# A decayed-attention and routed-expert kernel: compare table built group by group, ranks counted by matmuls, expert pieces at fixed steps, weights loaded one piece per step

## Chip, cores and metric

The kernel runs on one core of one Trainium2 chip. The metric is the device time in microseconds (us). Five engines work side by side, each through its own instructions in order: PE (TensorE, matmuls and transposes, with PEld for its weight loads), DVE (VectorE), ACT (ScalarE), POOL (GpSimd) and SP, which here only issues transfers (DMA). An instruction that needs another engine's result waits on a semaphore, and everything behind it on the same engine waits with it.

## The reference, cut to what matters

Four batches (B=4), eight heads (H=8), S=768 positions, head width 64, blocks of 64 positions.

```python
for b in range(nb):                                  # blocks of 64 positions
    intra = einsum('bhic,bhjc->bhij', qb, kb) * Dmask   # scores, decayed by lam
    intra = einsum('bhij,bhjd->bhid', intra, vb)
    inter = einsum('bhid,bhde->bhie', qb * lam_pow, kv_state)
    out[:, :, sl] = intra + inter
    kv_state = lam_block * kv_state + einsum('bhsd,bhse->bhde', kb * rev_pow, vb)
# x = out as (B, S, 512); then, per batch:
scores = einsum('bsd,d->bs', x, w_gate)
top_idx = argpartition(-scores[b], 128)[:128]        # the 128 best of 768 rows
ye = maximum(x[b, top_idx] @ w1, 0) @ w2             # 512 -> 1024 -> 512
out[b, top_idx] = x[b, top_idx] + sigmoid(scores)[:, None] * ye
```

All of it is in float32 in the kernel, but for small 0/1 tables.

## The kernel before

The work comes in 24 groups of 128 rows, six per batch (NT=6); a loop makes one **step** per group. F(g) below is the moment at which step g's first matmul, `from_scores(g)`, starts on PE.

Step g holds, in program order: loads of group g+6 (three DMAs of 256 KB, L67, on SP); in steps 0 to 3 two pieces of the expert weights of 512 KB each (`load_weights`, L83 and L86, on SP too); `from_scores(g)` and `outputs(g)` (PE writes the last part of group g, three ACT copies take it to `x_b`, SP stores it, L260); `from_states(g+1)`, `scores(g+1)` and `state_products(g+2)` on PE; `masked(g+1)` and two `next_state` on DVE, each fed by a `decayed` on POOL (L206): the state is a chain DVE, POOL, DVE, POOL through all groups of a batch; `gate_scores(g)` on DVE (L267); the transposes of group g+3 on PE with their ACT copies; `kd` (L143) and `qs` (L163) on POOL. Scores and state products share one PSUM tile `su`, of which there is one; the transposes and all expert results share two PSUM banks (`ps_m`).

When a batch's six groups are done, its routing begins: `rows` transposes all gate scores into one row (L288), `count` compares that row with each of the six score columns on DVE (`cmp`, L305, 128x768, six per batch) and sums up the ranks, `place_of_slots` makes a 0/1 table on DVE (`pick`, L330) and turns it into the 128 row numbers by six small matmuls (L337) and three DVE instructions. `fetch` gathers the rows from the output in memory by an indirect DMA on POOL's queue (L353). The expert is then `gate` (transposes L363), two `hidden` (L392) and `back` (L403), which ends in an indirect DMA that scatters the rows (L412, POOL).

`plan(b)` lays these pieces into later steps, where they stand between the two transposes of the step:

```python
s = (b + 1) * NT + (b < B - 1)
for i, piece in enumerate(counts):
    put(s + i // 2, piece)
s += 2
s = max(s, busy_until[0]); put(s + 1, where); put(s + 2, fetch)
for j, piece in enumerate(pieces):                 # gate, hidden, hidden, back
    put(s + 3 + j, piece)
```

So batch 0 counts in steps 7 to 9, places in 10, fetches in 11 and computes in 12 to 15; batch 1 does the same six steps later; batch 2 fetches in step 23 and computes after the loop; batch 3 does all of it after the loop. The expert's last `back` is written as one piece of eight matmuls.

## Time and profile before

| what | value |
|---|---|
| time, median of 3 runs (lowest, highest) | 235.78 us (235.48, 237.22) |
| the profiled execution: its time, its span in the trace | 238.65 us, 236.9 us |
| mean granted clock of TensorE, share of full speed | 0.848 |
| PE / PEld / DVE / ACT / POOL busy | 167.9 / 137.0 / 103.7 / 65.9 / 107.2 us |
| moved by DMA | 32.24 MB |

Busy times of engines overlap, so they don't add up to the span. A profile row of the timeline reads: start in us, duration in us, engine, source line, operation, what is written from what, count, and in brackets how long the engine sat idle before it and what ended that.

### The profile page before, as it was taken

The page shows a single profiled execution, that of the slowest core. Times are in us where ns is not written, and L with a number is a line of the kernel's source. Part 1 is how long each engine was busy: PE and PEld are TensorE (multiplying, and loading weights), DVE is VectorE, ACT ScalarE, POOL GpSimd, SP SyncE. Part 2 cuts the span into 40 slices and gives each one's busy share as a digit, 9 for nine tenths or more (in the row PEclk, how much of TensorE's full clock was granted, in tenths as well). Part 3 has the DMA queues.
Part 4 walks back from the last instruction along what each step waited for, and adds up shares of the span by engine and source line. Part 5 has one row for each costly group of instructions (what it writes and reads, how often), then busy time and mean ns, then how long its engine had stood idle before and what let it go on. Part 6 is the DMA issues. An engine that isn't in the chain of part 4 may idle for free.

```text
span 236.9 us, 7953 instructions
## 1 busy us (share of the span) xinstructions
PE 167.9 (71%) x3520; PEld 137.0 (58%) x3520; DVE 103.7 (44%) x241; ACT 65.9 (28%) x145; POOL 107.2 (45%) x105
## 2 busy tenths in 40 slices
PE   1869775775178519399999394999991499607991
PEld 1658665664167419298965293889651396207940
DVE  3545441253056983544852734348636180301001
ACT  2333351333043404243342133434311111001100
POOL 1689873656345972946461829664112000220001
PEclk9997997789558976959999869599998579965999
DMA  6999999999899998976573832101102200020001
GB/s 128 220 226 202 203 294 269 237 270 273 212 249 249 244 255 202 230 158 136 136 159 67 191 78 91 45 7 47 47 3 93 84 3 0 0 89 1 3 0 44
DMA packets 80962, 32.24 MB, mean 136 GB/s; under 512 B 75680, under 2 KB 75680, under 8 KB 80928
## 3 DMA queue, kind: packets, MB, share of 16 engines
q1 hardware_dynamic: 80144, 29.63, 53.6%
q0 software_dynamic: 640, 2.10, 3.0%
q8 instruction: 28, 0.46, 0.8%
q14 instruction: 6, 0.05, 0.1%
q10 hardware_dynamic: 144, 0.00, 0.0%
HBM read 24.38 MB, written 7.34 MB: 134 GB/s over the span
## 4 chain that ended last, share of the span: by engine, by line
PE 43%; DMA 21%; issue 13%; DVE 12%; POOL 6%; SPq 2%; ACT 1%; POOLq 1%
DMA kn<-in_k_dram 15%; PE ph L392 10%; PE py L403 9%; DMA xs<-out_dram,tok 6%; PE po L243 4%; PE su L196 4%; PE su L176 4%; DVE cmp L305 4%; PE tp_kT L154 3%; PE po L230 3%; POOL decayed L206 3%; PE tp_qT L154 2%; POOL kd L143 2%; DVE pick L330 2%; DVE p L183 2%
## 5 line engine op out<-in xcount | busy, mean ns | idle before, releaser
L206 POOL TENSOR_TENSOR decayed<-state,decay 128x256 f32<-128x256 f32 x40 | 39.6, 989 | 38.5 <-DVE state L217 32.5
L183 DVE TENSOR_TENSOR p<-su,mask 128x512 f32<-128x512 f32 x24 | 16.6, 691 | 42.0 <-PE su L196 37.0
L143 POOL TENSOR_TENSOR kd<-kn,kpow 128x512 f32<-128x512 f32 x24 | 27.3, 1136 | 16.2 <-DMA kn<-in_k_dram 16.1
L392 PE MATMUL ph<-xsT,w_sb 128*128 128x128 f32 x256 | 32.7, 292 | 1.0 <-ACT xsT L367 1.0
L392 PEld LDWEIGHTS ph<-xsT,w_sb 128*128 128x128 f32 x256 | 32.0, 208 | 1.8 <-ACT xsT L367 1.4
L412 POOL DMA_INDIRECT out_dram<-y,tok x4 | 5.5, 1386 | 60.6 <-DVE y L408 60.6
L163 POOL TENSOR_TENSOR qs<-qT,qpow 128x512 f32<-128x512 f32 x24 | 31.3, 1306 | 3.5 <-ACT qT L158 2.5
L305 DVE SCALAR_TENSOR_TENSOR cmp<-sc_row,sc,earlier 128x768 f32<-128x768 f32 x24 | 28.5, 1229 | 9.7 <-ACT sc_row L293 9.7
L158 ACT COPY qT<-tp_qT 128x512 f32<-128x512 f32 x24 | 14.1, 586 | 60.7 <-PE tp_qT L154 60.7
L403 PE MATMUL py<-w_sb,hs 128*128 128x512 f32 x64 | 28.2, 594 | 0.0
L154 PE MATMUL tp_qT<-ident,qn 128*128 128x128 f32 x96 | 19.2, 332 | 10.1 <-DMA qn<-in_q_dram 10.0
L217 DVE TENSOR_TENSOR state<-su,decayed 128x256 f32<-128x256 f32 x40 | 16.8, 419 | 21.2 <-POOL decayed L206 21.2
L230 PE MATMUL po<-state,qs 64*64 64x64 f32 x704 | 19.6, 237 | 7.9 <-issue 7.8
L176 PE MATMUL su<-qT,kT 64*64 64x64 f32 x768 | 21.1, 249 | 5.4 <-DVE state L217 4.0
L176 PEld LDWEIGHTS su<-qT,kT 64*64 64x64 f32 x768 | 18.1, 159 | 6.8 <-issue 6.6
L230 PEld LDWEIGHTS po<-state,qs 64*64 64x64 f32 x704 | 16.6, 152 | 8.8 <-issue 8.5
L196 PE MATMUL su<-vn,kd 64*64 64x64 f32 x704 | 21.0, 257 | 0.4 <-issue 0.3
L158 ACT COPY kT<-tp_kT 128x512 f32<-128x512 f32 x24 | 14.1, 587 | 20.7 <-PE tp_kT L154 20.5
L243 PE MATMUL po<-vn,p 64*64 64x64 f32 x768 | 18.9, 244 | 1.3 <-DVE p L183 1.3
L403 PEld LDWEIGHTS py<-w_sb,hs 128*128 128x128 f32 x64 | 11.8, 190 | 13.5 <-issue 13.4
L154 PEld LDWEIGHTS tp_qT<-ident,qn 128*128 128x128 f32 x96 | 12.5, 168 | 12.2 <-issue 10.4
L267 DVE CUSTOM_DVE_ANT_0 xg<-x_b,wg_b 128x512 f32<-128x512 f32 x24 | 18.8, 785 | 1.3 <-ACT x_b L259 1.3
(52 smaller groups left out, 164.4 us busy)
## 6 DMA issues: line engine op xcount, KB each, us to landing
qn<-in_q_dram SPq DMA_DIRECT2D x24, 256.0 KB, 4.9
kn<-in_k_dram SPq DMA_DIRECT2D x24, 256.0 KB, 5.2
vn<-in_v_dram SPq DMA_DIRECT2D x24, 256.0 KB, 5.2
out_dram<-x_b SPq DMA_DIRECT2D x24, 256.0 KB, 3.9
w_sb<-in_moe_w_dram SPq DMA_DIRECT2D x8, 512.0 KB, 5.8
wg_b<-in_moe_w_gate_dram SPq DMA_DIRECT2D x1, 256.0 KB, 5.2
xs<-out_dram,tok POOLq DMA_INDIRECT x4, 3.7
out_dram<-y,tok POOLq DMA_INDIRECT x4, 3.5
```

The lines of the kernel that those rows point to most:

```text
L143: nc.gpsimd.tensor_tensor(out=kd[:], in0=loaded[g][1][:], in1=kpow[:].rearrange("p a b -> p (a b)").unsqueeze(2).broadcast_to([128, H, D]) ...
L154: nc.tensor.transpose(tp[:, hp, :], in_=t[:, 2 * hp : 2 * hp + 2, :], identity=ident[:])
L158: nc.scalar.copy(out=dst[:], in_=tp[:])
L163: nc.gpsimd.tensor_tensor(out=qs[:], in0=qTs[g][:], in1=qpow[:].rearrange("p a c i -> p a (c i)"), op=ALU.mult)
L176: nc.tensor.matmul(su[half[c], hh, 0, hp, :], lhsT=kT[half[hh], hp, half[c]], rhs=qT[half[hh], hp, half[c]], start=True, stop=True, skip_g ...
L196: nc.tensor.matmul(su[half[hh], c, 1, hp, :], lhsT=kd[half[c], h, :], rhs=vn[half[c], h, :], start=True, stop=True, skip_group_check=True,)
L206: nc.gpsimd.tensor_tensor(out=t[:], in0=states[n][:], in1=decay[:], op=ALU.mult)
L230: nc.tensor.matmul(po[half[hh ^ c], hh, hp * D : (hp + 1) * D], lhsT=qs[half[hh], hp, half[c]], rhs=states[n][half[hh], hp, :], start=(hp ...
L243: nc.tensor.matmul(po[half[hh ^ c], hh, hp * D : (hp + 1) * D], lhsT=p[half[c], hh, hp, :], rhs=vn[half[c], 2 * hp + hh, :], start=(hp == ...
L305: nc.vector.scalar_tensor_tensor(out=cmp[:], in0=keep["sc_row"][:], scalar=scs[b][:, t : t + 1], in1=earlier[:, (NT - 1 - t) * L : (NT - 1 ...
L392: nc.tensor.matmul(ph[:, i, :], lhsT=w1_sb[:, dc, fs], rhs=xsT[:, dc, :], start=(dc == 0), stop=(dc == NDC - 1),)
L403: nc.tensor.matmul(py[:], lhsT=hs[:, fc, :], rhs=w2_sb[:, fc, :], start=(fc == 0), stop=(fc == NFC - 1),)
```

## The change

It does the following.

- **Routing.** `row(g)` transposes one group's gate scores in every step and ACT copies them into the row tile; `compare(g-1)` on DVE fills that group's part of a 0/1 table `wins` (bf16) against all groups so far, two instructions for the group itself and two more that grow with t, the number of groups before it. `places(b)` sums the table by twelve matmuls with a tile of ones (384 columns each, in two halves) and finds the row numbers with two DVE instructions of 384 elements and a small one. `count`, `place_of_slots` and their tables are gone.
- **Plan.** Pieces stand at fixed steps: for batches 0 to 2 with s=6(b+1): places and fetch in step s+1, gate in s+3, hidden in s+4 and s+5, `back`, now cut into two halves of four matmuls, in s+6 and s+7. For batch 3 places and fetch are in step 24, the rest behind it, two steps after. Steps past 23 come after the loop; there, batch 2's halves of `back` stand before and after batch 3's places.
- **Weights.** One piece of 512 KB per step in steps 1 to 8 in place of two per step in steps 0 to 3.
- **PSUM.** Scores move into the tile `po` of their own group (two of these); state products get a tile `pu`, which also holds the new row transpose. The two shared banks are handed out in turn, and one of them is held from the first half of `back` to the second.
- **Order.** `scores` now stand before `from_states`; `keys_decayed(g+3)` (`kd`) moves from between the two `decayed` of a step to the end of POOL's step.

```diff
+    def row(g, u):
+        b, t = divmod(g, NT)
+        ...
+        pb = u[:, 0, 256 : 256 + L]
+        nc.tensor.transpose(
+            pb, in_=scs[b][:, t : t + 1].broadcast_to([128, 128]), identity=ident[:]
+        )
+        nc.scalar.copy(out=rows_[b][:, t * L : (t + 1) * L], in_=pb)
+    def compare(g):
+        ...
+        nc.vector.scalar_tensor_tensor(
+            out=tie[:], in0=sc_row[:, here], scalar=s, in1=behind[:],
+            op0=ALU.is_le, op1=ALU.mult,
+        )
+        nc.vector.scalar_tensor_tensor(
+            out=wins[:, t, here], in0=sc_row[:, here], scalar=s, in1=tie[:],
+            op0=ALU.is_lt, op1=ALU.max,
+        )
+        if t > 0:
             nc.vector.tensor_scalar(
+                out=wins[:, t, : t * L], in0=sc_row[:, : t * L], scalar1=s, scalar2=None,
+                op0=ALU.is_lt,
+            )
             nc.vector.tensor_tensor(
+                out=wins[:, :t, here], in0=sc_row[:, here].unsqueeze(1).broadcast_to([128, t, L]),
+                in1=sc[:, :t].unsqueeze(2).broadcast_to([128, t, L]), op=ALU.is_le,
+            )
+    def places(b):
+        ...
+        for f in range(2):
+            cnt = bank([128, W], "cnt")
             for t in range(NT):
                 nc.tensor.matmul(
+                    cnt[:], lhsT=ones[:], rhs=wins_[b][:, t, f * W : (f + 1) * W],
                     start=(t == 0), stop=(t == NT - 1),
                 )
+                nc.vector.scalar_tensor_tensor(
+                    out=hit[:], in0=cnt[:], scalar=slot[:, i : i + 1],
+                    in1=token[:, f * W : (f + 1) * W],
+                    op0=ALU.is_equal, op1=ALU.mult, accum_out=part[:, f, i : i + 1],
+                )
     def plan(b):
-        s = (b + 1) * NT + (b < B - 1)
+        last = b == B - 1
+        s = (b + 1) * NT
+        put(s + (not last), lambda: places(b))
         for i in range(NGR):
             s = max(s, busy_until[0])
+            fetch, pieces = expert(b, i)
+            put(s + 1 - last, fetch)
             for j, piece in enumerate(pieces):
+                put(s + 3 - last + j, piece)
+            busy_until[0] = s + len(pieces)
     for g in range(NG):
-        for i in range(2 * g, min(2 * g + 2, n_w)):
-            load_weights(i)
+        if 0 < g <= n_w:
+            load_weights(g - 1)
         if g + 2 < NG:
             decay_state(2 * g + 4)
-        if g + 3 < NG:
-            keys_decayed(g + 3)
         from_scores(g)
         outputs(g)
         if g + 1 < NG:
+            scores(g + 1)
             from_states(g + 1)
         ...
+        if g > 0 and NGR:
+            compare(g - 1)
         if g + 3 < NG:
             transposes(g + 3, "qT", qTs)
             queries_decayed(g + 3)
+            keys_decayed(g + 3)
         for piece in later.pop(g, []):
             piece()
+        u = us.pop(g + 2)
+        if NGR:
+            row(g, u)
         if g + 3 < NG:
             transposes(g + 3, "kT", kTs)
```

Where batch 0's expert ends and batch 1's gather stands, on POOL in step 13 of the changed kernel (`tok_1197` are batch 0's row numbers, `tok_1941` batch 1's; the rows go from step 13 into step 14):

```order
L220 TENSOR_TENSOR decayed<-state,decay 128x256 x2
L174 TENSOR_TENSOR qs<-qT,qpow 128x512
L154 TENSOR_TENSOR kd<-kn,kpow 128x512
L425 DMA out_dram<-y,tok_1197 768x512
L361 DMA xs<-out_dram,tok_1941 128x512
L220 TENSOR_TENSOR decayed<-state,decay 128x256 x2
```

Before, two steps lay between batch 0's scatter (768x512, step 15) and batch 1's gather (step 17), as POOL's rows from one to the other show:

```order
L412 DMA out_dram<-y,tok 768x512
L143 TENSOR_TENSOR kd<-kn,kpow 128x512
L206 TENSOR_TENSOR decayed<-state,decay 128x256
L163 TENSOR_TENSOR qs<-qT,qpow 128x512
L206 TENSOR_TENSOR decayed<-state,decay 128x256
L143 TENSOR_TENSOR kd<-kn,kpow 128x512
L206 TENSOR_TENSOR decayed<-state,decay 128x256
L163 TENSOR_TENSOR qs<-qT,qpow 128x512
L353 DMA xs<-out_dram,tok 128x512
```

Now the gather is issued right behind the scatter, with nothing between them, and the next step's `decayed` stands behind both.

PE's last rows before, from the last group's `from_scores` (`po`, L243) on, are these; both the transposes `pt` and all matmuls `ph` and `py` of batches 2 and 3 come after it, with the six small matmuls of batch 3's `pick` (one pair of rows shown) between them:

```order
L243 MATMUL po<-vn,p 64x64 x16
L363 MATMUL pt<-ident,xs 128x128 x4
L288 MATMUL pb<-ident,sc 128x128 x6
L392 MATMUL ph<-xsT,w_sb 128x128 x32
L403 MATMUL py<-w_sb,hs 128x512 x8
L337 LDWEIGHTS pick
L337 MATMUL pe<-place,pick 128x2
```

The same place in the change (`po`, L252, is the last group's `from_scores`):

```order
L252 MATMUL po<-vn,p 64x64 x16
L400 MATMUL ph<-xsT,w_sb 128x128 x16
L295 MATMUL pu<-ident,sc 128x128
L413 MATMUL py<-w_sb,hs 128x512 x4
L334 LDWEIGHTS ones
L334 MATMUL cnt<-wins,ones 128x384
```

Batch 2's gate and first half of `ph` have moved ahead of the last group, into the loop, and the counting of batch 3 (twelve such pairs of `ones` and `cnt`) stands behind the first half of batch 2's `py`.

## Rows read from the trace of the kernel before

**Rows 1.** The page: the span, and busy time of each engine.

```profile
span 236.9 us, 7953 instructions
PE 167.9 (71%) x3520; PEld 137.0 (58%) x3520; DVE 103.7 (44%) x241; ACT 65.9 (28%) x145; POOL 107.2 (45%) x105
```

**Rows 2.** Windows: stretch, length, busy PE PEld DVE ACT POOL, clock, DMA share, GB/s.

```profile
35.00:69.00 34.00, 19.15 (x534) 16.34 (x530) 9.98 (x24) 9.95 (x23) 17.84 (x18) 0.75 0.99 253
69.00:94.00 25.00, 16.83 (x530) 15.22 (x534) 17.86 (x33) 8.78 (x21) 13.85 (x11) 0.79 1.07 241
...
107.00:130.00 23.00, 22.64 (x411) 17.71 (x410) 12.37 (x25) 8.04 (x17) 11.36 (x10) 1.00 0.58 126
...
154.00:181.00 27.00, 23.66 (x452) 18.49 (x455) 16.24 (x33) 7.60 (x17) 9.33 (x8) 0.99 0.12 42
```

**Rows 3.** Timeline of SP's queue: the issue of batch 0's last store.

```profile
64.60 1.00 SPq L260 DMA_DIRECT2D out_dram<-x_b  x1
```

**Rows 4.** DMA view, 35 to 70 us: issuer, count, KB each, median us to landing.

```profile
out_dram<-x_b SPq DMA_DIRECT2D x6, 256.0 KB, 4.9
```

**Rows 5.** Timeline of POOL: `kd` of groups 7 and 10, and one beside DVE.

```profile
37.48 1.04 POOL L143 TENSOR_TENSOR kd<-kn,kpow 128x512 f32<-128x512 f32 x1 [0.94 <-DMA kn<-in_k_dram]
...
63.26 1.04 POOL L143 TENSOR_TENSOR kd<-kn,kpow 128x512 f32<-128x512 f32 x1 [5.79 <-DMA kn<-in_k_dram]
...
80.93 1.76 POOL L143 TENSOR_TENSOR kd<-kn,kpow 128x512 f32<-128x512 f32 x1
```

**Rows 6.** Page's costliest groups: busy us, mean ns of one, idle before.

```profile
L206 POOL TENSOR_TENSOR decayed<-state,decay 128x256 f32<-128x256 f32 x40 | 39.6, 989 | 38.5 <-DVE state L217 32.5
L143 POOL TENSOR_TENSOR kd<-kn,kpow 128x512 f32<-128x512 f32 x24 | 27.3, 1136 | 16.2 <-DMA kn<-in_k_dram 16.1
L163 POOL TENSOR_TENSOR qs<-qT,qpow 128x512 f32<-128x512 f32 x24 | 31.3, 1306 | 3.5 <-ACT qT L158 2.5
L305 DVE SCALAR_TENSOR_TENSOR cmp<-sc_row,sc,earlier 128x768 f32<-128x768 f32 x24 | 28.5, 1229 | 9.7 <-ACT sc_row L293 9.7
```

**Rows 7.** Timeline of DVE: compares beside POOL and alone, smallest instruction, last gate score.

```profile
79.76 2.03 DVE L305 SCALAR_TENSOR_TENSOR cmp<-sc_row,sc,earlier 128x768 f32<-128x768 f32 x1
...
176.45 1.01 DVE L305 SCALAR_TENSOR_TENSOR cmp<-sc_row,sc,earlier 128x768 f32<-128x768 f32 x1
...
181.16 0.16 DVE L344 SCALAR_TENSOR_TENSOR tok_f<-ext 128x1 f32<-128x1 f32 x1
...
182.78 0.69 DVE L267 CUSTOM_DVE_ANT_0 xg<-x_b,wg_b 128x512 f32<-128x512 f32 x1 [1.27 <-ACT x_b L259]
```

**Rows 8.** Timeline of PE: starts of steps 12, 13, 15, 23, and pieces.

```profile
93.79 0.69 PE L243 MATMUL po<-vn,p 64*64 64x64 f32 x32
...
102.54 1.13 PE L243 MATMUL po<-vn,p 64*64 64x64 f32 x32
...
106.95 3.74 PE L392 MATMUL ph<-xsT,w_sb 128*128 128x128 f32 x32
...
118.95 0.69 PE L243 MATMUL po<-vn,p 64*64 64x64 f32 x32
...
121.47 7.03 PE L403 MATMUL py<-w_sb,hs 128*128 128x512 f32 x16
...
136.20 0.32 PE L337 MATMUL pe<-place,pick 128*128 128x2 bf16 x6 [3.75 <-DVE pick L330]
...
180.86 0.69 PE L243 MATMUL po<-vn,p 64*64 64x64 f32 x32
```

**Rows 9.** Timeline behind the loop: batch 2's scatter, batch 3's gather, first and last use.

```profile
206.06 1.46 POOL L412 DMA_INDIRECT out_dram<-y,tok  x1 [23.31 <-DVE y L408]
...
210.04 0.97 POOL L353 DMA_INDIRECT xs<-out_dram,tok  x1 [2.52 <-issue]
...
213.46 1.11 PE L363 MATMUL pt<-ident,xs 128*128 128x128 f32 x4 [6.45 <-DMA xs<-out_dram,tok]
...
231.69 0.75 DVE L408 SCALAR_TENSOR_TENSOR y<-py,g,xs 128x512 f32<-128x512 f32 x1 [15.65 <-PE py L403]
```

More of the change, by code (lines that the diff above doesn't have):

```diff
@@ L127, with bank @@
     nc.vector.tensor_copy(decay[:], qpow[:, :, 0, C - 1 : C].broadcast_to([128, NHP, D]))
-    qTs, qss, kTs, kds, ps_, sus = {}, {}, {}, {}, {}, {}
+    qTs, qss, kTs, kds, ps_, pos, us = {}, {}, {}, {}, {}, {}, {}
     states, decayed = {}, {}
+    banks, held = ["pm0", "pm1"], []
+    def bank(shape, name, hold=False):
+        tag = next(t for t in banks if t not in held)
+        banks.remove(tag)
+        banks.append(tag)
+        if hold:
+            held.append(tag)
+        return ps_m.tile(shape, FP32, name=name, tag=tag)
     x_bs, scs = {}, {}
@@ L315, in steps @@
             nc.vector.tensor_scalar(
-                out=scs[b][:], in0=scs[b][:], scalar1=2.0 ** -100, scalar2=2.0 ** -100,
-                op0=ALU.add, op1=ALU.subtract,
-            )
-        first = [steps] + [rows(t0, min(n, NT - t0)) for t0 in range(0, NT, n)]
-        return keep, first, [count(t) for t in range(NT)]
-    def expert(b, r0, keep):
-        n_in = min(128, CAP - r0)
-        def place_of_slots():
-            rank = keep["rank"]
-            pick = mod.tile([128, NT, 128], BF16, name="pick")
+                out=wins[:, t, : t * L], in0=sc_row[:, : t * L], scalar1=s, scalar2=None,
@@ L351, in fetch, with expert, rows_at @@
+        toks[b] = const.tile([128, NGR], I32, name=f"tok{b}")
+        nc.vector.scalar_tensor_tensor(
+            out=toks[b][:], in0=part[:, 0], scalar=float(b * S), in1=part[:, 1],
+            op0=ALU.add, op1=ALU.add,
+        )
+    def expert(b, i):
+        n_in = min(128, CAP - i * 128)
+        keep = {}
+        def rows_at():
+            return bass.IndirectOffsetOnAxis(ap=toks[b][:, i : i + 1], axis=0)
         def fetch():
@@ L397, in hidden, with back, do @@
             return do
[L399 to L416 removed]
+        def back(f0):
+            def do():
+                if f0 == 0:
+                    keep["py"] = bank([128, HD], "py", hold=True)
+                hs, py = keep["hs"], keep["py"]
+                for fc in range(f0, f0 + 4):
+                    nc.tensor.matmul(
+                        py[:], lhsT=hs[:, fc, :], rhs=w2_sb[:, fc, :],
+                        start=(fc == 0), stop=(fc == NFC - 1),
+                    )
+                if f0 + 4 < NFC:
+                    return
+                held.clear()
+                y = mod.tile([128, HD], FP32, name="y")
+                nc.vector.scalar_tensor_tensor(
+                    out=y[:], in0=py[:], scalar=keep["g"][:], in1=keep["xs"][:],
+                    op0=ALU.mult, op1=ALU.add,
+                )
+                nc.gpsimd.indirect_dma_start(
+                    out=rows_upto(b), out_offset=rows_at(), in_=y[:], in_offset=None,
+                )
+            return do
         return (
[L419 to L420 removed]
+            fetch,
+            [gate] + [hidden(f) for f in range(0, NFC, 4)] + [back(f) for f in range(0, NFC, 4)],
         )
```

216 lines of the change are left out of this document (71 added, 145 removed).

## The prediction

> **What bounds the kernel now.** The page comes first: no engine is busy for more than 71% of the span, so the waits decide, and they differ by stage [rows 1]. The windows show three stages [rows 2]. From 35 to 69 us the DMA share is 0.99 at 253 GB/s while PE works 19 of 34 us: loads bound it. POOL's timeline says the same: `kd` of group 10 stood 5.79 us until the keys landed at 63.3 us [rows 5]. From 69 to 94 us DVE is the fullest engine (17.9 of 25 us), with six `cmp` for one batch in steps 7 to 9, and PE is at 0.79 of its clock. Behind that, expert pieces make PE the bound: 22.6 of 23 us from 107 to 130, at the full clock; between such stretches PE stands for the row numbers, once for 3.75 us before `pe` [rows 2, 8]. The last group starts at 180.86 us [rows 8]; what follows to the end, 56.0 us, is a single file: batch 2's expert, then batch 3's. Gather to first use takes 3.4 us, the first `pt` to `y` 18.2 us, `y` to the end of the span 5.2 us [rows 1, 9].
>
> So I split the span at F(12)=93.8 and F(23)=180.9 us [rows 8], and work out the three parts anew.
>
> **What the steps cost.** Step 15 reaches `py` 2.5 us after its start with five of its six groups of PE work done; a sixth of like size makes about 3.0 us for a step at the full clock. Step 13 took 4.4 us for the same five, at the lower of the two levels of the clock (1.2 of 2.4 GHz): about 5.3 us for six [rows 8]. A `hidden` is 3.74 us with its last record's modelled end, 3.6 without, half a `py` 3.5 us (half of 7.03) [rows 8]. POOL's own work in a step is two `decayed`, a `qs` and a `kd`: 2 x 0.99 + 1.31 + 1.14 = 4.4 us, and between the `decayed` now stands nothing but DVE's wait for the first and its addition, some 0.5 us (estimate, from the line in the next paragraph at 256 elements): 5 us a step, where before `kd` filled that gap [rows 6].
>
> The new DVE work is not in the trace. The smallest DVE instruction took 0.16 us, a `cmp` of 768 elements 1.01 us [rows 7]; on the line through both, `tie` and `wins` (128 elements) are 0.3 us each, and the two that grow are 0.16 + 0.14 t each: 0.6 us for t=0, 2.3 us for t=5, 9.4 us for a batch, 37.6 us in all. Eight `hit` at 0.6 to 0.7 us add 5.3 us. Against them 28.5 us of `cmp` go [rows 6], and `pick` with its small ones: DVE gains at most 14.4 us, 0.6 us a step, hidden where DVE has room, as it has outside 69 to 94 us [rows 2]. A counting matmul of 384 bf16 columns lies between 0.05 us (0.32 us for six `pe`) and 0.44 us (7.03 us for sixteen records of `py`, 512 columns each) [rows 8]; I take 0.2 us, nearer to the lower, since bf16 needs no second record. Twelve are 2.4 us per batch, 0.6 to 5.3.
>
> **Part 1, up to F(12): 93.8 to about 90 us.** At 253 GB/s a 512 KB piece costs 2.1 us, a group's loads with one store (1 MB) 4.2 us [rows 2]. Ahead of group 10's keys stood eight pieces, now three: they land 10.4 us earlier, at 52.9 us instead of 63.3 [rows 5]. From there the queue brings a group every 4.2 + 2.1 = 6.3 us: group 11 at 59.2, group 14 at 78.1 us. If only loads bound, F(12) would be at 78.1 + 0.5 + 3.6 + 0.7 = 83 us.
>
> But the gather of batch 0 now stands on POOL in step 7, and it must wait for the store of group 5. That store was issued at 64.60 us [rows 3]; three pieces fewer ahead make 58.3 us, plus 4.9 us to land [rows 4]: 63.2 us. The row numbers are ready at about 57.5 us (52.9, transposes 0.5, counting 2.4, two `hit` and a small one 1.5). POOL stands some 6 us, then issues for 1.0 us [rows 9]. Behind it are `decayed` (1.0 us), the state on DVE (0.4, by the line above) and `gate_scores` (0.8 [rows 7]); the new `row(8)` on PE waits for that, until 66.5 us, seven after group 11 has landed. PE, idle, falls to the lower clock: F(9)=67.5 us, step 9 with the gate 6.6, step 10 with `hidden` 8.9, step 11 at the full clock 6.8 us: F(12)=89.8 us. Term: -4.0.
>
> **Part 2, F(12) to F(23): 87.1 to 70.7 us.** Steps 12, 16, 17 and 18 carry one piece: 3.0 + 3.5 + 0.2 (`row`) = 6.7 us each, 26.8. Step 13 ends batch 0's expert and fetches for batch 1. The second half of `back` ends at F+6.0, `y` at F+6.9, and the first counting matmul waits for it, since it writes the bank that `y` reads. POOL issues the scatter, and the gather behind it waits until that has landed: 3.98 us from issue to issue behind the loop [rows 9], so F+10.9, done at F+11.9. `decayed`, state and gate score again take 2.4 us, and `row(14)` goes at F+14.3, where PE has stood since F+12.5: F(15)=F+15. Step 15 takes POOL's 5 us or less: 19.6 us for three steps. Steps 19 to 21 are the same, 19.0 us without the last transposes. Step 22: 1.5 + 3.6 + 0.2 = 5.3 us. Sum 70.7, F(23)=160.5 us. Term: -16.4. What it saves is the place where PE waited for `cmp` and `pick`; it also takes up batch 2's gate and one `hidden`.
>
> **Part 3, F(23) to the end: 56.0 to about 38 us.** `from_scores` and batch 2's second `hidden` end at 4.3 us, ACT's two copies let `compare(23)` start at 5.3; it ends at 7.6 beside half of `py` (to 8.4). Two times counting (1.2) and `hit` (0.7) with the small one and the hand-overs: 12.5 us. The gather follows at once, for batch 2's scatter now stands behind it: 3.4 us, 16.0. The other half of `py` hides there. Then 18.2 and 5.2 us as before [rows 9]: 39.4, less some 1.4 us, since PE comes from work, not from the 6.45 us of idling [rows 9]: 38.0. Term: -18.0.
>
> Sum: -38.4 us. The profiled execution took 238.65 us, 1.75 us more than its span: 200.2. The median of the runs, 235.78, lies 2.9 us under it: 197.4, say **198 us**.
>
> **Rivals.** (a) POOL is not in the way: store 5 lands before the row numbers are ready, and the scatter is done sooner. Then F(12)=83 us, and each batch change costs 3.5 us less: 198 - 6.8 - 7 = 184 us. For it: a store that meets no backlog lands sooner. Against: the DMA share is 1.07 from 69 to 94 us [rows 2], so there is a backlog.
>
> (b) Compares and POOL block one another in every step. A `cmp` took 2.03 us beside POOL and 1.01 us alone [rows 7], a `kd` 1.76 us there, 1.04 us elsewhere [rows 5]: about the length of the other is added to each. Six steps have no piece to cover it (8, 9, 14, 15, 20, 21); 1.9 us of compare on POOL's chain in each is 11 us: 209 us, and 213 with one step at the lower clock behind each of two such pairs. I put half of one such collision into the 5 us of a step, as the means in rows 6 hold those of before. The Trainium skill, "SBUF — State Buffer", section "Who interferes with whom", has a rule for this: a DVE instruction with two inputs in SBUF and a GpSimd instruction that reads SBUF exclude each other for a whole instruction. By that rule it is the 209 us; the 2.03 and 1.76 us agree with it.
>
> (c) The other side: `row` stops PE in every step, and PE stays at the lower clock from step 11 to the end. A step then takes 5.3 us for 3.0, over twelve steps 28 us, of which 12 lie in waits that I have counted; four `hidden` and four half `back` in them double, 28 us; behind the loop 25 us of PE work doubles: 198 + 69 = 267 us. It makes the kernel slower than now from the point where 55% of that work runs so. For it: the stretch from 35 to 69 us, full of waits, has 0.75. Against: 1.00 and 0.99 where pieces stand between the groups [rows 2], and `row` should stop PE for at most 1 us: a gate score is ready 2.6 us after `from_scores` begins (180.86 to 183.5) [rows 7, 8], and PE has 2.5 us of other work. The Trainium skill, "TensorE: Matmul & The Clock Gate", section "What's actually happening", has the lower level as the default that only activity lifts; 0.75 among waits and 1.00 among pieces agree.
>
> (d) The change doesn't bring the loads forward, because SP waits for results before each store: F(12) stays at 93.8, the time is 202 us. That lies in the forecast's own range.
>
> **How the numbers follow.** Forecast with its unknowns (counting -2 to +6 us over the loop and the tail, `hit`, hand-overs, (d)): 191 to 206 us, 0.56. (a), 184 to 191: 0.15. (b), 206 to 218: 0.20. (c) in full or in part: slower by over 1% 0.06, within 1% 0.03; 1% is about what a measurement of this kernel can tell from no change. The range of 186 to 214 us leaves out (c), 0.09, and the ends of (a) and (b), another 0.1. Faster: 0.91.
>
> **What would show it.** The first starts of `from_scores` for groups 12 and 23 give the three parts: 90, 160 and 38 us behind. `xs` of batch 0 on POOL idle before, till a store near 63 us; `xs` of batches 1 and 2 about 4 us behind the scatter; `row` waiting for DVE by about 2 us in steps 14 and 20. Wrong would be: a granted clock below 0.8 from 110 us on (c), `decayed` and compares long in all steps (b), no wait at the gathers (a), keys of group 10 not before 60 us (d).

## The result and the profile after

The changed kernel takes 210.0 us, the median of four runs (207.5 to 216.0), against 236.5 us for the kernel before beside it (235.5 to 237.7). The ratio is 0.879, with a 95% interval of 0.870 to 0.888: 12% faster. Two of the four runs of the changed kernel (211.7 and 216.0 us) were disturbed and are left out of the ratio, as are such runs in every ratio below, the profiled ones of `one compare instruction` and of `row` a step later among them. The profiled execution of the changed kernel took 207.49 us, with a span of 205.8 us, and the comparisons below start from it.

The page of the changed kernel, span and busy times, to be set beside [rows 1]; DVE works 28 us more than before, where the prediction had 14.4 us at most:

```profile
span 205.8 us, 8020 instructions
PE 161.9 (79%) x3544; PEld 129.4 (63%) x3544; DVE 131.7 (64%) x270; ACT 67.9 (33%) x161; POOL 101.0 (49%) x105
```

The page's chain of work that ended last, by engine, first of the kernel before and then of the changed one. Loads (DMA) have mostly left it; DVE and POOL have taken their place:

```profile
PE 43%; DMA 21%; issue 13%; DVE 12%; POOL 6%; SPq 2%; ACT 1%; POOLq 1%
```

```profile
PE 45%; DVE 22%; POOL 12%; issue 11%; DMA 5%; SPq 2%; POOLq 1%; ACT 0%; DVEq 0%; ACTq 0%
```

The windows of the changed kernel, columns as in [rows 2]: F(1) to F(7), F(7) to F(12), F(12) to F(19), F(19) to F(23), and the single file behind it. The early stretch, which had a clock of 0.75 from 35 to 69 us before, has 0.89, and DVE is the fullest engine in the first of these:

```profile
23.00:57.28 34.28, 23.71 (x791) 20.57 (x791) 26.69 (x48) 15.27 (x36) 22.26 (x23) 0.89 1.03 247
57.28:91.86 34.58, 28.43 (x734) 25.29 (x733) 28.38 (x54) 13.62 (x33) 21.69 (x22) 0.95 0.95 241
91.86:142.50 50.64, 44.29 (x1033) 35.19 (x1032) 38.96 (x71) 19.07 (x48) 29.23 (x29) 0.97 0.69 162
142.50:169.43 26.93, 23.66 (x542) 18.73 (x541) 18.89 (x43) 8.74 (x23) 10.56 (x11) 0.87 0.19 62
169.43:205.80 36.37, 28.45 (x178) 18.85 (x177) 8.15 (x21) 4.49 (x11) 2.98 (x3) 0.98 0.08 29
```

The two moments that split the span, from PE's timeline; they answer to the first and last of [rows 8]:

```profile
91.86 0.69 PE L252 MATMUL po<-vn,p 64*64 64x64 f32 x32
...
169.43 0.69 PE L252 MATMUL po<-vn,p 64*64 64x64 f32 x32
```

So the three parts are 91.9, 77.6 and 36.4 us, where 93.8, 87.1 and 56.0 were before. The time came from the end (19.7 us) and the middle (9.5 us); the front gave 1.9 us.

What DVE is doing is seen in step 5. These are DVE's and POOL's lines of one compare from the timeline; each of the first three compare instructions ends shortly after the POOL instruction beside it (0.15, 0.14 and 0.28 us), though the third has four times the elements of the first:

```profile
50.03 1.26 POOL L174 TENSOR_TENSOR qs<-qT,qpow 128x512 f32<-128x512 f32 x1
...
50.44 1.00 DVE L308 SCALAR_TENSOR_TENSOR tie<-sc_row,sc,behind 128x128 f32<-128x128 f32 x1
...
51.25 1.09 POOL L154 TENSOR_TENSOR kd<-kn,kpow 128x512 f32<-128x512 f32 x1
...
51.47 1.01 DVE L312 SCALAR_TENSOR_TENSOR wins<-sc_row,sc,tie 128x128 bf16<-128x128 f32 x1
...
52.30 0.78 POOL L220 TENSOR_TENSOR decayed<-state,decay 128x256 f32<-128x256 f32 x1
52.41 0.95 DVE L317 TENSOR_SCALAR wins<-sc_row,sc 128x512 bf16<-128x512 f32 x1
```

And the same two in the last compare, with POOL idle, and the page's groups of all 24 (busy us, mean ns):

```profile
174.71 0.35 DVE L308 SCALAR_TENSOR_TENSOR tie<-sc_row,sc,behind 128x128 f32<-128x128 f32 x1 [1.01 <-ACT sc_row L298]
175.10 0.35 DVE L312 SCALAR_TENSOR_TENSOR wins<-sc_row,sc,tie 128x128 bf16<-128x128 f32 x1
```

```profile
L308 DVE SCALAR_TENSOR_TENSOR tie<-sc_row,sc,behind 128x128 f32<-128x128 f32 x24 | 21.5, 895 | 1.0 <-ACT sc_row L298 1.0
L312 DVE SCALAR_TENSOR_TENSOR wins<-sc_row,sc,tie 128x128 bf16<-128x128 f32 x24 | 21.0, 876 | 0.8
```

Of each, 5 met no POOL instruction and took 0.35 us; 19 did and took 1.04 and 1.01 us on average. The Trainium skill, "SBUF — State Buffer", section "Who interferes with whom", says that a DVE instruction with two inputs in SBUF and a GpSimd instruction that reads SBUF shut each other out for a whole instruction; these rows agree, 0.35 against 1.00 us.

### The profile page after: what moved, and what is told of

Its sections match the earlier page's. It is cut to its first block, busy times and chain, and to the rows that moved or that the text cites. A ratio compares the mean times of both kernels' runs of the same rounds, so it can differ in the third digit from the quotient of the medians.

```text
span 205.8 us, 8020 instructions
## 1 busy us (share of the span) xinstructions
PE 161.9 (79%) x3544; PEld 129.4 (63%) x3544; DVE 131.7 (64%) x270; ACT 67.9 (33%) x161; POOL 101.0 (49%) x105
## 4 chain that ended last, share of the span: by engine, by line
PE 45%; DVE 22%; POOL 12%; issue 11%; DMA 5%; SPq 2%; POOLq 1%; ACT 0%; DVEq 0%; ACTq 0%
PE ph L400 11%; POOL decayed L220 8%; PE po L252 6%; DVE state L231 6%; PE py L413 5%; PE po L241 5%; PE po L187 5%; DVE wins L312 4%; PE tp_kT L165 4%; DVE tie L308 4%; PE cnt L334 3%; DVE p L194 3%; PE pu L210 3%; DMA kn<-in_k_dram 2%; PE tp_qT L165 2%
## 5 line engine op out<-in xcount | busy, mean ns | idle before, releaser
L220 POOL TENSOR_TENSOR decayed<-state,decay 128x256 f32<-128x256 f32 x40 | 35.8, 895 | 38.6 <-DVE state L231 31.2
L194 DVE TENSOR_TENSOR p<-po,mask 128x512 f32<-128x512 f32 x24 | 16.5, 686 | 17.9 <-PE po L241 17.9
L231 DVE TENSOR_TENSOR state<-pu,decayed 128x256 f32<-128x256 f32 x40 | 16.8, 420 | 16.5 <-POOL decayed L220 15.7
L295 PE MATMUL pu<-ident,sc 128*128 128x128 f32 x24 | 7.5, 311 | 21.9 <-DVE state L231 18.4
L210 PE MATMUL pu<-vn,kd 64*64 64x64 f32 x704 | 19.9, 241 | 3.7 <-issue 3.5
L308 DVE SCALAR_TENSOR_TENSOR tie<-sc_row,sc,behind 128x128 f32<-128x128 f32 x24 | 21.5, 895 | 1.0 <-ACT sc_row L298 1.0
L312 DVE SCALAR_TENSOR_TENSOR wins<-sc_row,sc,tie 128x128 bf16<-128x128 f32 x24 | 21.0, 876 | 0.8
L210 PEld LDWEIGHTS pu<-vn,kd 64*64 64x64 f32 x704 | 17.4, 154 | 4.7 <-issue 4.1
L187 PE MATMUL po<-qT,kT 64*64 64x64 f32 x768 | 18.8, 241 | 0.4 <-issue 0.4
L165 PE MATMUL tp_kT<-ident,kn 128*128 128x128 f32 x96 | 16.9, 305 | 2.1 <-DVE hit L340 1.8
L361 POOL DMA_INDIRECT xs<-out_dram,tok x4 | 4.1, 1021 | 29.4 <-DVE tok L346 25.5
```

What stands on the lines that cost most here:

```text
L165: nc.tensor.transpose(tp[:, hp, :], in_=t[:, 2 * hp : 2 * hp + 2, :], identity=ident[:])
L187: nc.tensor.matmul(po[half[c], hh, 1, hp, :], lhsT=kT[half[hh], hp, half[c]], rhs=qT[half[hh], hp, half[c]], start=True, stop=True, skip_g ...
L210: nc.tensor.matmul(us[g][half[hh], c, hp * D : (hp + 1) * D], lhsT=kd[half[c], h, :], rhs=vn[half[c], h, :], start=True, stop=True, skip_g ...
L220: nc.gpsimd.tensor_tensor(out=t[:], in0=states[n][:], in1=decay[:], op=ALU.mult)
L231: nc.vector.tensor_tensor(out=new[:], in0=u, in1=decayed.pop(n)[:], op=ALU.add)
L308: nc.vector.scalar_tensor_tensor(out=tie[:], in0=sc_row[:, here], scalar=s, in1=behind[:], op0=ALU.is_le, op1=ALU.mult,)
```

## The experiments

All times stand beside runs of the kernel before on the same chip. Compare the ratios and not the medians, for a median holds all runs. A ratio has an interval of about ±0.009, so those between 0.867 and 0.886 cannot be told from the changed kernel's 0.879. F(12), F(12) to F(23) and F(23) to the end are from the timeline of each profile, in us; each is a single execution.

| run | median us | ratio | F(12) | to F(23) | to end |
|---|---|---|---|---|---|
| changed kernel | 210.0 | 0.879 | 91.9 | 77.6 | 36.4 |
| two pieces a step | 209.0 | 0.886 | 96.7 | 74.4 | 36.2 |
| one compare instruction | 206.9 | 0.873 | 93.0 | 77.8 | 36.3 |
| `decayed` on ACT | 204.9 | 0.874 | 91.0 | 76.2 | 36.4 |
| `row` a step later | 213.9 | 0.910 | 96.5 | 80.6 | 36.5 |
| `row` in its own tile | 205.1 | 0.873 | 92.2 | 73.7 | 38.0 |
| `row` after the score only | 206.9 | 0.870 | 90.1 | 75.9 | 36.3 |
| fetch a step later | 215.1 | 0.914 | 97.4 | 78.4 | 38.0 |
| two-instruction compare, no `decayed` | 204.6 | 0.867 | 91.2 | 74.0 | 38.0 |
| combined, recurrence on DVE | 202.0 | 0.846 | 91.2 | 73.2 | 36.3 |
| combined, `decayed` on ACT | 205.2 | 0.862 | 90.8 | 76.1 | 36.3 |
| the same, keys first | 205.4 | 0.872 | 92.0 | 73.1 | 38.0 |

### Is it the loads?

Undoing the spread of the weights in the changed kernel, and doing it alone in the kernel before:

```diff
-        if 0 < g <= n_w:
-            load_weights(g - 1)
+        for i in range(2 * g, min(2 * g + 2, n_w)):
+            load_weights(i)
```

> The changed kernel with one part undone: two weight pieces in each of steps 0 to 3, as before the change, instead of one in steps 1 to 8. Theory A (the prediction's part 1: in steps 1 to 11 the loads set the pace, and spreading the pieces is what brings F(12) forward): the keys of group 10 come some 10 us later, POOL's `kd` stands for them again for over 5 us in steps 5 to 7, F(12) moves from 91.9 to 97-102 us and the time from 207.5 to 213-218 us. Theory B (the steps are set by the chain of DVE and POOL instructions, and the loads have slack even with two pieces a step): `kd` stands 0 to 2 us more, F(12) 91.9 to 94 us, time 207 to 210 us.

> The kernel before with this one part of the change alone: one weight piece a step from step 1 on. Theory A: the waits for keys (16.1 us in six places on POOL up to 95 us) go, F(12) comes some 8 to 11 us earlier than 93.8 us and the time falls from 236 to 225-229 us. Theory B: those waits go, but most of what they covered stands behind them (POOL's 4.4 us a step with DVE's compares), F(12) comes 2 to 5 us earlier, time 231 to 235 us.

In the changed kernel the undone spread costs 4.8 us at F(12), nearly what A expected, but of these 3.2 us are given back before F(23), and the ratio rises by 0.007: within what can be measured, as B expected. Of what came back, 1.1 us lie in step 14, where batch 1's gather was issued 3.61 us behind the scatter and not 4.91, 1.0 us in step 20, and 1.2 us in step 21, which ran for the most part at the lower level of the clock in the changed kernel and at the higher one here. The windows of that step, first of the changed kernel, then of this one (columns as in [rows 2]):

```profile
158.85:163.99 5.14, 4.99 (x119) 4.35 (x118) 3.52 (x9) 2.06 (x5) 1.24 (x2) 0.54 0.15 54
```

```profile
161.70:165.60 3.90, 2.88 (x118) 2.49 (x117) 3.85 (x9) 2.18 (x5) 1.80 (x3) 1.00 0.21 74
```

`kd` does not stand for its keys in either (4.9 us, all of it the first load). In the kernel before, the spread alone brings the ratio to 0.979 (0.971 to 0.987), 230.3 against 235.3 us, between the two forecasts; F(12) comes at 86.2 us instead of 93.8 (no expert piece stands ahead of it there), and POOL's waits for keys fall from 16.1 us [rows 6] to these, of which 4.9 us are again the first:

```profile
POOL kd L143 <- DMA kn<-in_k_dram: 8.2, 4, 4.9
```

So loads did bound the early steps before, for some 5 us of the time; in the changed kernel the same edit is worth some 2 us, which cannot be told from nothing.

### Is it the compares beside POOL?

```diff
-        tie = (row <= s) * behind;  wins = (row < s) max tie     # two instructions
+        wins = (row - s) < behind                                # one; behind holds 0 or 2**-100
```

> The changed kernel with `tie` and `wins` (two DVE instructions of 128 elements with two operands in SBUF each) made one: (row - own score) < a table that holds 0 where the other token stands ahead and a tiny number where it stands behind. Same table of wins. Theory L (a DVE instruction with two operands in SBUF waits for the POOL instruction under way, whatever its own size): 24 instructions of 0.85 to 0.9 us go, DVE's busy time falls from 131.7 by about 21 us to 111 us, the one that stays has a mean of 0.8 to 1.0 us, and the time falls by 3 to 8 us, since the steps without pieces hang on this chain. Theory S (the price is that of the operation, not of its neighbour on POOL): the one instruction does the work of both, its mean is 1.2 us or more, DVE stays within 10 us of 131.7 us, the time within 2 us.

The edit is shown in short form. The lines of DVE (mean ns behind busy us), of the two growing compares only the largest shape:

```profile
L307 DVE SCALAR_TENSOR_TENSOR wins<-sc_row,sc,behind 128x128 bf16<-128x128 f32 x24 | 19.6, 816 | 1.4 <-ACT sc_row L298 1.4
...
L316 DVE TENSOR_TENSOR wins<-sc_row,sc 128x640 bf16<-128x640 f32 x4 | 4.9, 1218 | 0.0
...
L312 DVE TENSOR_SCALAR wins<-sc_row,sc 128x640 bf16<-128x640 f32 x4 | 4.5, 1132 | 0.0
```

The one that stays has 0.82 us, as L expected, but DVE's busy time falls by 9 us only (131.7 to 122.7): the instructions behind it, 899 and 813 ns before the edit, now run beside POOL in its place and grow to 1132 and 1218 ns. The 1 us is therefore not a price per DVE instruction. It goes with POOL's own time: the next DVE instruction that meets `qs`, `kd` or `decayed` takes the wait over. Theory L holds as to the cause and fails as to the sum, and the 9 us of DVE's work bought no time that can be measured (0.873 against 0.879).

Taking work from POOL instead, by making `decayed` on ACT:

```diff
-        nc.gpsimd.tensor_tensor(out=t[:], in0=states[n][:], in1=decay[:], op=ALU.mult)
+        for hp in range(NHP):
+            nc.scalar.activation(t[:, hp, :], states[n][:, hp, :], AF.Copy, scale=decay[:, hp, 0:1])
```

> The changed kernel with `decayed` (40 POOL instructions of 0.9 us) made on ACT instead, as four instructions of 64 columns each; DVE's work is the same. Theory L (DVE's compare instructions and POOL's instructions shut each other out: 0.35 us alone, 1.04 us beside POOL for `tie`): with 36 us less on POOL, more of the 24 `tie` and 24 `wins` run alone, their 42.5 us fall to 25-33 us, DVE's busy time falls by 10 to 20 us and the time by 4 to 10 us. Theory N (they are long for another reason, such as reading what ACT has just written): they stay at 40 to 44 us. If ACT's own order then holds the recurrence up (`decayed` stands behind the copies of x_b and before that of qT), POOL's place is taken by ACT and the time is 207 to 215 us, with DVE's busy time down all the same.

The durations of `tie` and `wins` (minimum, median, maximum in ns):

```profile
L311 DVE SCALAR_TENSOR_TENSOR tie<-sc_row,sc,behind x24: 341/343/352, 26.5 to 172.5; 128x128 f32<-128x128 f32 x24
```

```profile
L315 DVE SCALAR_TENSOR_TENSOR wins<-sc_row,sc,tie x24: 352/1244/1315, 26.9 to 172.9; 128x128 bf16<-128x128 f32 x24
```

`qs` now waits for ACT's copy and starts behind the start of `tie` (54.89 against 54.72 us in step 6), so all 24 `tie` come first and take 0.34 us, and `wins` meets `qs` instead. The same instruction takes a third of its time with only its neighbour changed: theory N falls. Together the two fall to 34.7 us, just short of the 25 to 33 us that L gave, and DVE's busy time by 4 us instead of 10 to 20, for the reason of the run before: the wait moves on. The ratio is 0.874, not to be told from 0.879. So what the collisions cost the kernel is not shown by either run.

### Is it `row`?

PE's waits of the changed kernel, longest first, and what one of them looks like in step 14: the gate score is there at 113.43 us, `row` starts at 114.52, just behind the second `state`.

```profile
PE pu L295 <- DVE state L231: 18.4, 8, 3.8
```

```profile
113.35 0.08 DVE L276 DVE_READ_ACCUMULATOR2_ANT sc<- 128x1 f32 x1
...
114.04 0.42 DVE L231 TENSOR_TENSOR state<-pu,decayed 128x256 f32<-128x256 f32 x1 [0.61 <-POOL decayed L220]
...
114.52 0.32 PE L295 MATMUL pu<-ident,sc 128*128 128x128 f32 x1 [3.76 <-DVE state L231]
```

First edit: `row` of a group behind the next step's `from_scores`, with its tile `pu` kept until then.

```diff
         outputs(g)
+        if g > 0 and NGR:
+            row(g - 1, us.pop(g + 1))
...
-        u = us.pop(g + 2)
-        if NGR:
-            row(g, u)
```

> The changed kernel with `row` of a group moved on PE from the end of its step to the next step, behind that step's `from_scores`; the compare of that group stays where it is on DVE. PE's waits in front of `row` (20 us in 10 places over the whole) lose their cause. Theory P (the wait of `row` for DVE's state and gate score is itself on the path, as it keeps the transposes of keys and the next step from PE): the time falls by 8 to 15 us. Theory B (PE only waits there for a chain of DVE and POOL that would end no sooner): the wait moves to another matmul (`pu` of the next group, or `po` behind `p`), and the time falls by 0 to 3 us.

It is slower, 0.910: a case that neither theory had. `row` writes the bank that `state_products` of the new step need, so these now wait for ACT's copy of the row, and the copies stand in ACT's order. In step 10 ACT holds them for the expert's gate value:

```profile
78.88 0.20 ACT L384 ACTIVATE g<-g 128x1 f32<-128x1 f32 x1 [3.02 <-DVE g L380]
...
80.61 0.27 ACT L298 COPY sc_row<-pu 128x128 f32<-128x128 f32 x1
```

```profile
80.97 1.14 PE L210 MATMUL pu<-vn,kd 64*64 64x64 f32 x32 [3.33 <-issue]
```

The copy of the row ends at 80.88 us and PE starts at 80.97, though the profile names no releaser. This is no chance: in seven of the versions, the changed kernel among them, PE stands for a microsecond or more before this matmul in the step of a first `hidden`, eleven times in all, and each time it starts 0.09 to 0.10 us behind the end of ACT's copy. Here it stood 3.33 us, and the `hidden` behind it ran at the lower clock (5.7 us). Second edit: `row` stays, `pu` becomes two tiles.

```diff
-        us[g] = ps_u.tile([128, 2, 512], FP32, name="pu")
+        us[g] = [ps_u.tile([128, 512], FP32, name=f"pu{c}") for c in range(2)]
```

> The changed kernel with the PSUM tile `pu` split into one tile for each of its two banks, so that `row`, which writes the first bank, has no tie to the second `state`, which reads the other bank. Theory T (the wait of `row` for `state`, 18.4 us in 8 places, is due to the shared tile): `row` goes some 1.0 us sooner in steps without pieces, as soon as the gate score is there, and the time falls by 2 to 8 us. Theory B (DVE's order is what ends the step, and `row` waits for the gate score, which stands behind the first `state` on DVE anyway): the waits are relabelled or fall by less than 5 us in sum and the time by 0 to 2 us.

The wait is now for the score, and `row` follows it at once:

```profile
PE pu L295 <- DVE sc L276: 10.4, 11, 2.5
```

```profile
112.84 0.08 DVE L276 DVE_READ_ACCUMULATOR2_ANT sc<- 128x1 f32 x1
...
112.98 0.32 PE L295 MATMUL pu<-ident,sc 128*128 128x128 f32 x1 [1.93 <-DVE sc L276]
```

So the shared tile was the cause, as T said, and of the 20.0 us that PE waits for DVE before `row`, 9.6 go. Steps 13 to 15 take 20.9 us instead of 22.3, steps 19 to 21 19.4 instead of 21.5, and F(12) to F(23) 73.7 instead of 77.6 us. Not all of that is `row`: steps 14 and 20 fell by 1.8 and 2.0 us, and the clock in the two groups of steps was 0.97 and 1.00, where it had been 0.92 and 0.84. With two pieces a step and `row` as it was, the same groups took 20.9 and 19.3 us. The end is 1.6 us longer in this profile, and the ratio 0.873 is not certain to be lower. Third edit: besides, the gate score ahead of both `state` on DVE, and the expert's gate value made with the first half of `back`.

```diff
             masked(g + 1)
+        gate_scores(g)
...
-        gate_scores(g)
```

> The changed kernel with `pu` in two tiles as in the run before, the gate score of a group ahead of both `state` on DVE, and the expert's gate value (ACT's exp and three small ones on DVE) made with the first half of `back` instead of with the gate piece, where ACT's queue stood 3 us for DVE. So `row` waits for the copies of x_b and one DVE instruction alone. Theory R (what the prediction missed in the steps without pieces is that `row` ends behind both states, not behind the gate score): PE's waits before `row`, 20 us of the changed kernel, fall below 6 us, steps 13 to 15 take 19.6-21 us instead of 22.3, steps 19 to 21 19-20.5 us instead of 21.5, and the time falls to 199-203 us. Theory B (the recurrence through DVE and POOL sets the pace whatever `row` does): PE waits elsewhere (`pu` for `kd`, `po` for `p`), time 204 to 206 us.

Inconclusive: 0.870. The edit did not do what it was made for. The bank that `row` writes is the one that the first `state` reads, and with the score first this `state` stands behind it: in step 14 the score is there at 109.68 us, the first `state` ends at 111.73, and `row` starts right behind that:

```profile
111.79 0.32 PE L295 MATMUL pu<-ident,sc 128*128 128x128 f32 x1 [2.42 <-DVE state L231]
```

So PE's waits before `row` fell from 20.0 to 15.6 us only, and both `state`, with `decayed` on POOL (46.2 us of waiting, 38.6 in the changed kernel), come later. Theory R was not tested by it.

### Is it POOL at the gather?

```diff
-            put(s + 1 - last, fetch)
+            put(s + 2 - 2 * last, fetch)
```

> The changed kernel with the gathers of batches 0 to 2 issued one step later (the pieces stay where they are), so that the gather no longer follows the row numbers or the scatter of the batch before in the same step on POOL. Theory G (the prediction's steps 7, 13 and 19: POOL standing in front of the gather, 1.7, 3.9 and 2.5 us, holds up `decayed`, `state`, `row` and so PE): the steps 14 and 20 lose their long wait of `row`, the time falls by 4 to 7 us, from 207.5 to 201-204 us. Theory B (the steps beside it are set by DVE's own order): 0 to 2 us less. A loss is possible in the step behind, where the first `pt` now waits for a gather that was issued a step later (some 3.4 us from issue to use against a step of 6 us): at most 1 us each.

Slower, 0.914. The wait of POOL at the gather goes, but the loss was underestimated: the gather is issued at the end of POOL's step (74.80 us for batch 0), and the first `pt` of batches 0 to 2 waits for it, 2.9 to 3.3 us each, 9.5 us in all:

```profile
81.08 1.09 PE L371 MATMUL pt<-ident,xs 128*128 128x128 f32 x4 [3.34 <-DMA xs<-out_dram,tok]
```

Where the change had put the gather, POOL stands 8.1 us in three places; a step later, PE stands 9.5 us in three.

### DVE's order as a whole

The two-instruction compare (the one that grows, and one of 128 to 768 columns against the table) with the recurrence on DVE alone:

```diff
-            nc.vector.tensor_tensor(out=new[:], in0=u, in1=decayed.pop(n)[:], op=ALU.add)
+            for hp in range(NHP):
+                nc.vector.scalar_tensor_tensor(out=new[:, hp, :], in0=states[n][:, hp, :],
+                    scalar=decay[:, hp, 0:1], in1=u[:, hp, :], op0=ALU.mult, op1=ALU.add)
```

> The changed kernel with DVE's and POOL's chain shortened in two ways: a compare is two instructions instead of four (one of 128 to 768 columns against a table, and the one that grows), and the recurrence (state x decay + product) is made on DVE alone, four instructions of 64 columns each from PSUM, so that POOL's 40 `decayed` and two hand-overs per state go. Theory B (steps 1 to 23 are set by that chain): POOL's busy time falls from 101 to 65 us, the compares' from 77 us to 25-40 us, `state`'s rises from 17 to 28-36 us, and the time falls to 188-199 us. Theory A' (the loads, at a DMA share near 1 until 118 us, leave no room): F(12) stays within 2 us of 91.9 us and the time at 203 us or more.

POOL falls from 101 to 75 us, the compares from 68.9 to 48.7 (25 to 40 were expected), `state` costs DVE 33.9 us, and the time is 204.6 us, ratio 0.867 (0.858 to 0.876): above B's range. F(12) is 91.2 us, where A' wanted it. Together with the third edit on `row`:

> The run just before together with the two-instruction compare and the recurrence on DVE alone. If chain and `row` each cost what their own runs showed (3 us each against the changed kernel's 207.9 us), the sum gives 199 to 202 us; if they are the same time counted twice, 203 to 205 us; if the steps were bound by both in turn, so that only both together free them, 192 to 198 us, with F(12) at 84-88 us, near the 83 us at which the loads alone would put it.

202.0 us, ratio 0.846 (0.837 to 0.855): the one version that is certainly faster than the changed kernel, by some 4%. The two parts, 1.4% and 1.0% by themselves, add up, within their intervals, and F(12) stays at 91.2 us: up to F(9) 7 us are won (65.0 instead of 72.0 us), and steps 9 and 10 give all but 0.7 us back. The last two runs tried ACT for `decayed` in it, and then `kd` ahead of `qs`:

> As the combined kernel, but with `decayed` on ACT (four instructions of 64 columns) and the addition on DVE as in the changed kernel: DVE has 17 us less work than there, ACT 36 us more and a hand-over per state. If DVE's work sets the steps, this is 1 to 5 us faster than the other combined kernel; if the length of the recurrence does (state, hand-over, four instructions on ACT, hand-over, state), it is 1 to 5 us slower.

> The combined kernel with `decayed` on ACT, and on POOL `kd` ahead of `qs` (two lines exchanged): `kd` needs the loaded keys alone, and stood behind `qs`, which waits for ACT's copy of qT. In the run before, PE waited for `kd` 16.8 us in 13 places. If these waits are on the path, they go and the time falls from 203-206 us to 193-199 us, below the other combined kernel (202 us). If the recurrence through ACT or the length of the loads stands right behind them, the waits reappear at `p` or `state` and the time stays at 201 to 205 us.

```diff
-            queries_decayed(g + 3)
             keys_decayed(g + 3)
+            queries_decayed(g + 3)
```

Both stay behind the recurrence on DVE (0.862 and 0.872 against 0.846, where the first interval, 0.853 to 0.870, just touches that of 0.846), though DVE has 16 to 20 us less to do than there (105.8 and 109.7 against 125.7 us). So DVE's load alone does not set the time; that the length of the recurrence does, the other case of the expectation, is argued from this and not shown by itself. With the keys first, PE's 16.8 us of waits for `kd` go, and about the same time comes back as waits of `row` for `state` (15.6 us, from 4.4) and of `pt` for the gather (5.9 us, from 1.2). Here POOL's timeline also shows the store that the prediction spoke of. The last store of batch 0 was issued at 59.47 us and landed 5.4 us later, the row numbers were ready at 62.82 us, and the gather stood until 65.82 us, 0.95 us behind the landing (the profile names a load of the same queue as what ended the wait):

```profile
59.47 0.42 SPq L272 DMA_DIRECT2D out_dram<-x_b  x1
...
62.66 0.16 DVE L341 SCALAR_TENSOR_TENSOR tok<-part 128x1 int32<-128x1 f32 x1
```

```profile
65.82 1.55 POOL L356 DMA_INDIRECT xs<-out_dram,tok  x1 [4.62 <-DMA qn<-in_q_dram]
```

## Why the prediction was right, and where its sizes were off

The range, 186 to 214 us, holds the result; the forecast of 198 us was 12 us short of the median and 9.5 us short of the profiled execution, outside its own 191 to 206. The time lies in what rival (b) gave, 206 to 218 us: the range holds the result because that rival had a place in it, and the main line missed, by 6.9 us in part 2 alone.

**Part 1**, 91.9 us for 89.8. The landing of the loads was as told: the keys of group 10, issued at 45.86 us, landed 6.7 us later, at 52.6 us (52.9 forecast), no `kd` waits behind the first, and the last store of batch 0 went out at 58.53 us (58.3 forecast). The step that failed is the one after: the row numbers were to be ready at 57.5 us and the gather to wait for the store until 63.2. In the trace the numbers came last, at 66.03 us, and POOL stood for them:

```profile
65.87 0.16 DVE L346 SCALAR_TENSOR_TENSOR tok<-part 128x1 int32<-128x1 f32 x1
...
66.32 1.15 POOL L361 DMA_INDIRECT xs<-out_dram,tok  x1 [1.71 <-DVE tok L346]
```

The store had landed by then, at 64.4 us. Its issue, and its row in the DMA view of 58.5 to 58.6 us (the last number is the time from issue to landing, 4.9 in the forecast):

```profile
58.53 0.42 SPq L269 DMA_DIRECT2D out_dram<-x_b  x1
```

```profile
out_dram<-x_b SPq DMA_DIRECT2D x1, 256.0 KB, 5.9
```

So the store's wait, which was told right in its mechanism, was covered by 1.6 us. Where the numbers came sooner, it appeared: with the keys first, in the fastest version and with `row` a step later the gather was issued some 0.95 us behind the store's landing, and 3.0 to 4.0 us behind the numbers.

The numbers were late because of the pace of steps 1 to 6: 5.7 us each where POOL's own work would give 5, with no wait of `kd` for its keys among them. In step 5 DVE's chain is `state`, `tie`, `wins`, the two growing compares and `p`, one behind the other, and PE stands 1.0 to 2.6 us before `row` in each of these steps. Which of the two sets the pace is not shown, but the profiles speak for `row`: with the two-instruction compare and the recurrence on DVE these steps took 6.0 us each, with `row` in its own tile 5.6 and with `row` after the score only 5.4. That F(12) came within 2.1 us of the forecast is in part luck: F(9), at 72.0 us, was 4.5 us late, and step 9 then took 4.4 us where 6.6 were worked out at the lower clock.

**The compares** are the term that was mis-sized. Forecast were 37.6 us on DVE, hidden, with half of one collision in a step; measured are 68.9 us (`tie` 21.5, `wins` 21.0, the growing ones 14.4 and 12.0). Alone `tie` takes 0.35 us (0.3 forecast). So the line over the number of elements was right, and the cover was wrong: beside POOL, `tie` and `wins` take 1.04 and 1.01 us. That this made the kernel slower than forecast is not shown: 9 us and 4 us less of DVE's work left the ratio where it was, within what can be measured. The smaller terms hold: twelve counting matmuls 2.1 us (2.4), `hit` 0.62 us (0.6 to 0.7).

**Part 2**, 77.6 us for 70.7. The steps with one piece are as worked out: 6.59 us (12), 6.72 (17) and 6.60 (18) for 6.7, 5.44 (22) for 5.3. Step 16 took 8.44, and steps 13 to 15 took 22.3 us for 19.6 and 19 to 21 21.5 for 19.0. The gathers did stand behind the scatters, 4.91 and 3.56 us from issue to issue for the 3.98 forecast, though the row numbers were ready at 108.46 and 152.51 us:

```profile
105.72 1.04 POOL L425 DMA_INDIRECT out_dram<-y,tok  x1 [1.09 <-DVE y L421]
110.63 0.97 POOL L361 DMA_INDIRECT xs<-out_dram,tok  x1 [3.88 <-DVE p L194]
```

```profile
149.76 1.03 POOL L425 DMA_INDIRECT out_dram<-y,tok  x1 [1.09 <-DVE y L421]
153.32 0.97 POOL L361 DMA_INDIRECT xs<-out_dram,tok  x1 [2.53 <-DVE tok L346]
```

Three things were missed. `row` waits for both states, not for the gate score: 1.1 us in step 14. PE stood 3.76 us there, where the prediction had 1 to 2 us. And behind that stop PE ran at the lower level for much of the next step: the granted clock is 0.69 in step 15 and 0.54 in step 21, where the full one was taken. A stop of this length does not always bring that: with two pieces a step PE stood 2.19 us in step 20, longer than the 1.68 us of the changed kernel, and step 21 ran at 1.00:

```profile
161.00 0.32 PE L295 MATMUL pu<-ident,sc 128*128 128x128 f32 x1 [2.19 <-DVE state L231]
```

At 1.00, step 21 took 3.9 us there and 5.0 us with `row` in its own tile, for 5.14, so the price of the clock in it lies between nearly nothing and 1.2 us. With two pieces a step, with `row` in its own tile and with `decayed` on ACT the two groups take 18.9 to 20.9 and 19.3 to 19.9 us.

The third is ACT's order. In the step of a first `hidden` (10 and 16) ACT holds the copy of the row for the expert's gate value, and PE's state products, which need the bank, start 0.10 us behind that copy; in step 16 this is 1.48 of the 1.7 us over the forecast:

```profile
123.39 0.20 ACT L384 ACTIVATE g<-g 128x1 f32<-128x1 f32 x1 [2.80 <-DVE g L380]
123.50 0.25 ACT L298 COPY sc_row<-pu 128x128 f32<-128x128 f32 x1
...
123.85 0.69 PE L210 MATMUL pu<-vn,kd 64*64 64x64 f32 x32 [1.48 <-issue]
```

Where the gate value is made later, this stop is gone, but step 16 still takes 8.0 to 9.1 us: something else stands right behind it. What is left of the 6.9 us was not taken apart.

**Part 3**, 36.4 us for 38.0. The gather of batch 3 comes 12.0 us behind F(23) (12.5), 3.6 us pass to the first `pt` (3.4), and from there `y` follows after 15.6 us where 18.2 less 1.4 were taken: PE comes from work and stays at 0.98 of its clock. No run undid the plan or the counting alone, so what each of them gave of the 29 us in parts 2 and 3 is read from the traces and not shown by an experiment.

**Rivals.** (a): its condition came true, the store landed before the row numbers were ready, but because the numbers were late; its price fell, for POOL stood at all three gathers, 1.7, 3.9 and 2.5 us. (b): the collisions happened, in all steps rather than in six, and the time lies in its range, but no run shows that they made it. (c) falls as a whole: the granted clock is 0.94 on the mean, and 0.87 from 142 to 169 us. In small it is there, in steps 15 and 21. (d) falls as worded, since the loads came forward; undoing that costs 4.8 us at F(12), near its price of 4 us, of which some 2 us reach the end.

## What to carry to other kernels

Before costing new DVE work as hidden, look at which POOL instructions stand beside it in each step: here small ones with two operands in SBUF took about as long as their neighbour on POOL, and merging them, or moving a part of POOL's work, shifted that wait to the next one. And less work on an engine is not less time: 9 us less on DVE left the time of the kernel where it was, within what can be measured. Where a small PE instruction shares a tile with another result, look up what else reads that tile before you say for what it will wait, and what stands ahead of the copy that frees it. When an early bound is lifted, ask what stands second: here it gave the changed kernel 2 us at the front, while the single file at the end gave 20.

## What the runs showed of the hardware that was not expected

F(12) lies between 90.1 and 93.0 us in all versions of the changed kernel but three, though F(9) ranges from 65.0 to 72.4 us in these. In part this is the store and the gather above (8.5 us from the gather to its data with the keys first, at a DMA share of 0.94). In part it is a stop of PE in step 10. In the changed kernel this is 1.65 us, ending at 79.67 us, and it is the wait for ACT's copy of the row that was told above, which ends at 79.57 us. In the fastest version, where the gate value is made later, another stop stands in its place, and it falls between two matmuls of one group of four transposes of the same tile:

```profile
74.58 0.33 PE L165 MATMUL tp_qT<-ident,qn 128*128 128x128 f32 x1
...
78.52 0.80 PE L165 MATMUL tp_qT<-ident,qn 128*128 128x128 f32 x3 [3.62 <-issue]
```

With `row` after the score only there is one of 1.22 us inside `hidden`, ending at 78.73 us. No row ends these two. A packet of the queue that the page calls "instruction" moved between 74 and 80 us in both, but also in the two combined versions with `decayed` on ACT, which have no such stop, so what they are stays open. It also stays open whether the loads set F(12): the DMA share is 1.00 over the first 91.9 us of the changed kernel, at 232 GB/s, though neither `kd` nor a transpose stands for keys or queries behind the first.
